# Laying q and k token by token on GpSimd before the DMA transposes of a fused attention and feed-forward kernel

## The chip, the cores and the metric

The kernel runs on one NeuronCore of a Trainium2 chip. The metric is the device time of one execution in microseconds (us), and of several executions the median counts. The engines are named as in the profile: PE is the tensor engine's matmuls and PEld its weight loads, DVE the vector engine, ACT the scalar engine, POOL is GpSimd, and SP is the engine that issues DMAs here, the transposing ones among them. An engine with a q behind its name (SPq) means its sequencer.

## The reference

For 8 batches, 12 heads, 448 tokens and a head width of 64, the kernel computes attention without a softmax, followed by a feed-forward block with a layer norm in front and a residual:

```python
scores = scale * np.matmul(q, k.transpose(0, 1, 3, 2))
attn = np.maximum(scores, 0.0) ** 2 / S
x = np.matmul(attn, v)                      # then heads side by side: (8, 448, 768)
xn = (x - mu) / np.sqrt(var + 1e-06) * g_ln
out = x + np.maximum(xn @ w_ch1, 0.0) @ w_ch2   # 768 -> 3072 -> 768
```

## The kernel before

**Groups.** A batch's twelve heads make six head pairs, and two head pairs (r = 0 and 1) make a group, so a batch has three groups (`G`) and the kernel 24. `load` brings q, k and v of a group in by a DMA issued on POOL, as tiles of 128 partitions (head of the pair, 64 token rows) by two times 448 elements. The 448 elements are seven tokens (`J`) of 64 elements, so a token and a head pair have a chunk of 64 columns each.

**Transposes.** The scores need q and k with the head width on the partitions. Batches 0 and 1 are transposed on PE (`transposes`). Batches 2 to 7 (groups 6 to 23, since `by_dma` is 2) are transposed by DMAs that SP issues, in blocks of 128 columns. A block of k holds two neighbouring chunks of one head pair (or, at the seam, the last of one pair and the first of the other), and they land on the partitions 0 to 63 and 64 to 127. The partner of a chunk of k is q's seven chunks of the same head pair on the same partitions, which is not where a plain transpose leaves all of them. So q is transposed twice, the second time shifted by 64 columns: `keys_dma` transposes 7 blocks of k (L227), `queries_dma` 8 blocks and 7 shifted blocks of q (L232 and L233), 22 blocks in three instructions a group. For the shift, q of batches 2 to 7 (and of batch 0) lies in `qbuf`, three fixed tiles with 64 columns of zeros on both sides (L101 to L104).

**Order.** The order of the instructions on each engine is the order in which the program writes them (a manual schedule): each engine takes its own in turn, and semaphores hold an instruction back until its inputs are there and its output buffer is free. After a start with batches 0 and 1 interleaved with their feed-forward part, the kernel goes through pairs of batches. `ffn1` (L479) of a pair runs alone; `ffn2` (L514) of that pair is interleaved with the attention of the next pair (`attention`, L408): between stretches of `ffn2` matmuls stands a bundle of three `item`s, each of which is the score matmuls (L270) of a group for one of its seven key blocks, and in some bundles also `product` of the group before (attention times v, L296). There are three such attention stages, 107 to 181, 236 to 312 and 367 to 441 us.

For each item ACT takes the ReLU out of the accumulator (L281) and DVE squares it (L282). After `product`, DVE scales the result (L303) and multiplies it by the gain (L309), and POOL adds up the chunks for the layer norm's mean (L324 and L327 in `chunks_summed`, and at a batch's end the conversion L330 and the subtraction L331). `centre` turns the sum into the mean on PE (L344), ACT copies it (L348) and DVE subtracts it (L350) in front of `ffn1`.

**In an attention stage, `transposed(n+1)` (L356) is called at the first item of group n.** It issues the loads of k for group n+4 and of q for group n+3, then the two transposes of q for group n+1 and the transpose of k for group n+2. The result of `queries_dma` has two buffers, that of `keys_dma` three. On SP these DMAs stand in one queue with the output DMAs (L529) and with `tokens` (L451), which transposes the attention's result of a pair, 42 blocks in one instruction.

Of the kernel before, what the change touches and what calls it, by code (L numbers as in the profile page):

```python
# [28 lines left out]
def kernel(  # L29
# [32 lines left out]
    J = S // HP  # L62
    NP = H // 2
    G = NP // 2
    NB = 2 * J + 1
    K1 = d_model // P
    K2 = d_ff // P
    S2 = 2 * S
# [7 lines left out]
    const = ctx.enter_context(tc.tile_pool(name="const", bufs=1))  # L76
# [21 lines left out]
        for n, t in (("q", q), ("k", k), ("v", v))  # L98
    }
    qkv = {}  # L100
    qbuf = [const.tile([P, 2 * S + 2 * D], bf16, name=f"q_sb{i}") for i in range(3)]  # L101
    for t in qbuf:
        nc.vector.memset(t[:, :D], 0.0)
        nc.vector.memset(t[:, D + 2 * S:], 0.0)  # L104

    groups = [(b, m) for b in range(B) for m in range(G)]

    def load(n, names):
        if n >= len(groups):
            return  # L110
        b, m = groups[n]
        for name in names:
            if b == 1 and name != "v":
                o = (2 * m + "qk".index(name)) * 2 * S
                t = hold[:, o:o + 2 * S].rearrange("p (r s) -> p r s", r=2)
            elif name == "q":
                t = qbuf[m][:, D:D + 2 * S].rearrange("p (r s) -> p r s", r=2)
            else:
                t = io.tile([P, 2, S], bf16, tag=name, name=name + "_sb", bufs=4 if name == "v" else 3)
            nc.gpsimd.dma_start(t, srcs[name][b][:, m:NP:G, :])  # L120
            qkv[name, b, m] = t
# [35 lines left out]
    ones = const.tile([P, P], bf16)  # L157
# [22 lines left out]
    def transposes(b, m):  # L180


        if b == 0:
            o = 12 * 1024 + m * 2 * J * P
            sb = early[:, o:o + 2 * J * P].rearrange("p (i c) -> p i c", c=P)
        elif m:
            o = (m - 1) * 2 * J * P
            sb = hold[:, o:o + 2 * J * P].rearrange("p (i c) -> p i c", c=P)
        else:
            sb = tpool.tile([P, NB, P], bf16, tag="qT", name="qT_sb")  # L190
        for i, n in enumerate(("q", "k")):
            src = qkv[n, b, m]
            if (b, m) == (0, 0):
                idle((36, 4)[i])
            if b == 0:
                ps = ps_mm.tile([P, 1024], bf16, tag="mm", name="tr_ps")
            else:
                ps = ps_sc.tile([P, 2, 1024], bf16, tag="sc", name="tr_ps")[:, 0]
            for j in range(J):
                for pr in range(2):  # L200
                    nc.tensor.transpose(  # L201
                        ps[pr * HP:(pr + 1) * HP, j * P:(j + 1) * P],
                        src[:, pr, j * D:(j + 1) * D], identity)
# [13 lines left out]

    kts = {}

    def keys_dma(n):
        if n >= len(groups):
            return
        kts[n] = tpool.tile([P, J, P], bf16, tag="kT", name="kT_sb", bufs=3)
        nc.sync.dma_start_transpose(kts[n], qkv[("k",) + groups[n]].rearrange("p r s -> p (r s)"))  # L227

    def queries_dma(n):
        m, kt = groups[n][1], kts[n]  # L230
        qt = tpool.tile([P, NB, P], bf16, tag="qT", name="qT_sb")
        nc.sync.dma_start_transpose(qt[:, 0:2 * J + 1:2, :], qbuf[m][:, :])  # L232
        nc.sync.dma_start_transpose(qt[:, 1:2 * J:2, :], qbuf[m][:, D:D + 2 * S])  # L233

        def queries(i, r):
            o = (2 * i + r) // J * J + 1 - r
            return qt[:, o:o + J]
        st[groups[n]] = {
            "q": queries,
            "k": lambda i: kt[:, i],  # L240
            "where": lambda pr, j: divmod(pr * J + j, 2),
            "attn": []}


# [6 lines left out]
    def busy(n):  # L251


        ps = ps_mm.tile([P, 512], fp32, tag="mm", name="busy_ps")
        for _ in range(n):
            nc.tensor.matmul(ps[:, :S], ones, qbuf[0][:, D:D + S], start=True, stop=True)

    def of(blk, b=0):
        o = b % 2 * S
# [2 lines left out]
    def scores(n, slots, blk):  # L262
        g, w = st[groups[n]], blk[1] * HP
        ps = ps_sc.tile([P, 2, 512], fp32, tag="sc", name="sc_ps")
        for o, i in enumerate(slots):
            for r in range(2):
                rows = slice(r * HP, (r + 1) * HP)
                for hh in range(2):
                    cols = slice(hh * HP, (hh + 1) * HP)
                    nc.tensor.matmul(  # L270
                        ps[cols, r, o * w:(o + 1) * w], g["k"](i)[rows, cols],
                        g["q"](i, r)[rows, blk[0]:sum(blk), cols], start=True, stop=True)
        if groups[n][0]:
            a = apool.tile([P, 2, 512], bf16, tag="attn", name="attn_sb")
        else:
            o = n_early[0] % 12 * 1024
            a = early[:, o:o + 1024].rearrange("p (r s) -> p r s", r=2)
            n_early[0] += 1
        since[0] = 0
        a = a[:, :, :len(slots) * w]  # L280
        nc.scalar.activation(a, ps[:, :, :len(slots) * w], ACTF.Relu)  # L281
        nc.vector.tensor_mul(a, a, a)  # L282
        for o, i in enumerate(slots):
            g["attn"].append(a[:, :, o * w:(o + 1) * w])
# [69 lines left out]
    by_dma = 2  # L354

    def transposed(n):  # L356

        if groups[n][0] < by_dma:
            transposes(*groups[n])
            return  # L360


        if n == by_dma * G:
            keys_dma(n)
        else:
            if n == by_dma * G + 1:
                load(n + 2, "k")
            load(n + 3, "k")
            load(n + 2, "q")
        queries_dma(n)  # L370
        keys_dma(n + 1)

    def attention_block(b, blk):

# [33 lines left out]
    def attention(bs):  # L408

        lo, hi = bs[0] * G, (bs[-1] + 1) * G
        seq = [(n, i) for n in range(lo, hi) for i in range(J)]

        def item(n, i):
            if i == 0 and n + 1 < len(groups) and groups[n + 1][0] >= by_dma:
                transposed(n + 1)  # L420
            scores(n, (i,), FULL)

        def product(n):
            values(n, FULL)
# [136 lines left out]
    interleave(ffn1_units(0, BLK[0][1]), attention_block(1, BLK[1][0]), 3, 1)  # L561
    interleave(ffn1_units(1, BLK[1][0]), attention_block(1, BLK[1][1]), 3, 1)
    tokens(0)
    for unit in ffn1_units(1, BLK[1][1]):
        unit()
    statistics(0, 0)
# [42 lines left out]
```

## Time and profile before

| | |
|---|---|
| median of the three runs | 557.33 us (556.60 to 557.53) |
| the profiled execution's own time | 557.41 us |
| its span, first to last instruction | 555.6 us |
| PE busy | 537.8 us, 97% of the span |
| DVE, ACT, POOL busy | 266.9, 257.8, 110.4 us |
| matmuls of `ffn2`, `ffn1`, scores of batches 2 to 7 | 227.4, 219.6, 34.8 us |
| granted tensor clock | 0.998 |

The busy times are the union of an engine's instructions. A group of instructions is told as line, engine, operation, output and inputs with their shapes, the count, then busy time and the mean duration of one, then the time that the engine sat idle just before them and what ended the idle time. The chain of work that ended last is followed back from the last instruction. The timeline gives start and duration of merged neighbours. A DMA has a second time, the one at which its data have landed.

### The profile page before, as it was taken

The numbers are of one execution on the slowest core, as the hardware profiler recorded it, in microseconds if no ns is written. First come the engines' busy times: TensorE is split into PE (matmuls) and PEld (weight loads), VectorE is DVE, ScalarE is ACT, GpSimd is POOL, SyncE is SP. The second block draws the span as 40 slices with busy tenths as digits, with TensorE's granted clock in tenths as the row PEclk, the third lists the DMA queues.
The fourth block names the chain that finished last, engine by engine and source line by source line (L and its number), as shares of the span: only waits on it lengthen the run. The fifth ranks groups of instructions, "written<-read, shape, count | busy, mean of one in ns | idle before, by whom it ended". The sixth has DMA issues, their size and how long they took to land.

```text
span 555.6 us, 10931 instructions
## 1 busy us (share of the span) xinstructions
PE 537.8 (97%) x4718; PEld 315.7 (57%) x4718; DVE 266.9 (48%) x510; ACT 257.8 (46%) x418; POOL 110.4 (20%) x136
## 2 busy tenths in 40 slices
PE   6879999999999999999999999999999999999996
PEld 5568778855555555555545555555555555556563
DVE  4856754178897350047777523016687670001111
ACT  4666766465643444455445344445555244430000
POOL 8334102014523310002524401001230400000000
PEclk9999999999999999999999999999999999999999
DMA  9999997969998990008998892005951240001122
GB/s 147 207 204 208 211 189 106 148 101 152 141 167 130 133 131 0 1 19 150 136 159 143 110 164 34 0 1 83 164 112 29 57 102 0 1 0 39 48 57 58
DMA packets 106896, 56.16 MB, mean 101 GB/s; under 512 B 77152, under 2 KB 103264, under 8 KB 106848
## 3 DMA queue, kind: packets, MB, share of 16 engines
q0 software_dynamic: 27520, 25.96, 32.7%
q1 hardware_dynamic: 79328, 29.51, 32.0%
q8 instruction: 37, 0.61, 0.4%
q14 instruction: 11, 0.09, 0.0%
HBM read 51.91 MB, written 11.01 MB: 113 GB/s over the span
## 4 chain that ended last, share of the span: by engine, by line
PE 91%; DMA 3%; ACT 2%; DVE 2%; SPq 0%; issue 0%; POOL 0%; POOLq 0%
PE o_ps L514 39%; PE h_ps L479 38%; PE sc_ps L270 6%; PE av_ps L296 5%; DMA qT_sb<-q_sb 2%; ACT early L281 2%; PE h_ps L498 1%; DMA k_sb<-in_k_dram 1%; PE sum_ps L344 1%; DVE early L282 1%; PE tr_ps L201 1%; DVE early L208 0%; SPq L232 0%; DVE o_sb L520 0%; DVE hT_sb L484 0%
## 5 line engine op out<-in xcount | busy, mean ns | idle before, releaser
L514 PE MATMUL o_ps<-w,hT_sb 128*128 128x384 bf16 x1344 | 227.4, 327 | 0.0
L479 PE MATMUL h_ps<-xc_sb,w 128*128 128x448 bf16 (+2 forms) x1368 | 219.6, 318 | 6.2 <-DVE hT_sb L484 5.3
L514 PEld LDWEIGHTS <-hT_sb 128*128 128x128 bf16 x1344 | 127.7, 98 | 97.5 <-issue 16.1
L479 PEld LDWEIGHTS <-w 128*128 128x128 bf16 x1368 | 128.5, 98 | 93.3 <-issue 10.0
L281 ACT ACTIVATE attn_sb<-sc_ps 128x896 bf16<-128x896 f32 (+4 forms) x150 | 126.5, 902 | 84.9 <-PE sc_ps L270 84.9
L486 ACT ACTIVATE hT_sb<-h_ps 128x448 bf16<-128x448 f32 (+2 forms) x212 | 102.5, 483 | 127.2 <-PE h_ps L479 126.7
L282 DVE TENSOR_TENSOR attn_sb<-attn_sb 128x896 bf16<-128x896 bf16 (+4 forms) x150 | 94.8, 640 | 54.2 <-ACT attn_sb L281 52.8
L520 DVE SCALAR_TENSOR_TENSOR o_sb<-o_ps,rstd_sb,xtok_sb 128x384 f32<-128x384 f32 x56 | 34.2, 611 | 55.6 <-PE o_ps L514 55.6
L464 DVE RECIPROCAL rstd_sb<-rstd_sb 128x1 f32<-128x1 f32 (+1 forms) x10 | 1.7, 169 | 96.6 <-ACT rstd_sb L463 96.6
L327 POOL TENSOR_TENSOR part_sb<-part_sb,xT_sb 128x448 f32<-128x448 f32 x24 | 29.5, 1229 | 71.1 <-DVE xT_sb L303 63.5
L458 DVE BATCH_NORM_STATS2 stats<-xtok_sb 128x6 f32<-128x384 bf16 x56 | 27.5, 533 | 33.4 <-DMA xtok_sb<-xT_sb 33.4
L350 DVE SCALAR_TENSOR_TENSOR xc_sb<-total_sb,g_mean,xc_sb 128x448 bf16<-128x448 f32 (+2 forms) x54 | 29.0, 606 | 21.1 <-ACT total_sb L348 21.1
L270 PE MATMUL sc_ps<-qT_sb,kT_sb 64*64 64x448 bf16 x504 | 34.8, 357 | 1.4 <-DMA qT_sb<-q_sb 1.4
L324 POOL TENSOR_TENSOR part_sb<-xT_sb 128x448 f32<-128x448 bf16 x6 | 6.6, 1105 | 140.3 <-DVE xT_sb L303 120.0
L296 PE MATMUL av_ps<-attn_sb,v_sb 64*64 64x448 bf16 (+2 forms) x672 | 32.1, 327 | 0.0
L309 DVE TENSOR_SCALAR xc_sb<-xT_sb,g_sb 128x448 bf16<-128x448 bf16 (+2 forms) x58 | 28.8, 544 | 1.0
L120 POOL DMA_DIRECT2D k_sb<-in_k_dram x21 | 15.1, 719 | 71.6 <-DMA kT_sb<-k_sb 40.3
L303 DVE TENSOR_SCALAR xT_sb<-av_ps 128x896 bf16<-128x896 f32 (+2 forms) x30 | 27.0, 899 | 4.5 <-PE av_ps L296 4.5
L296 PEld LDWEIGHTS <-v_sb 64*64 64x64 bf16 x840 | 22.8, 107 | 10.4 <-issue 2.0
L120 POOL DMA_DIRECT2D v_sb<-in_v_dram x24 | 17.5, 732 | 26.2 <-PE av_ps L296 23.9
L270 PEld LDWEIGHTS <-kT_sb 64*64 64x64 bf16 x504 | 11.5, 106 | 18.3 <-issue 14.9
L281 ACT ACTIVATE early<-sc_ps 128x768 bf16<-128x768 f32 (+3 forms) x24 | 18.3, 823 | 3.0 <-PE sc_ps L270 2.9
(56 smaller groups left out, 163.3 us busy)
## 6 DMA issues: line engine op xcount, KB each, us to landing
out_dram<-o_sb SPq DMA_DIRECT2D x56, 192.0 KB, 2.9
v_sb<-in_v_dram POOLq DMA_DIRECT2D x24, 224.0 KB, 4.6
q_sb<-in_q_dram POOLq DMA_DIRECT2D x21, 224.0 KB, 7.3
k_sb<-in_k_dram POOLq DMA_DIRECT2D x21, 224.0 KB, 6.3
w<-in_moe_w_ch_dram POOLq DMA_DIRECT2D x12, 384.0 KB, 14.5
w<-in_moe_w_ch_dram POOLq DMA_DIRECT2D x4, 1152.0 KB, 19.6
hold_sb<-in_q_dram POOLq DMA_DIRECT2D x3, 224.0 KB, 11.9
hold_sb<-in_k_dram POOLq DMA_DIRECT2D x3, 224.0 KB, 11.1
```

The source lines that it names most:

```text
L120: nc.gpsimd.dma_start(t, srcs[name][b][:, m:NP:G, :])
L270: nc.tensor.matmul(ps[cols, r, o * w:(o + 1) * w], g["k"](i)[rows, cols], g["q"](i, r)[rows, blk[0]:sum(blk), cols], start=True, stop=True)
L281: nc.scalar.activation(a, ps[:, :, :len(slots) * w], ACTF.Relu)
L282: nc.vector.tensor_mul(a, a, a)
L296: nc.tensor.matmul(ps[cols, hh, :w], v_sb[rows, pr, j * D:(j + 1) * D], g["attn"][i][rows, r, :], start=(j == 0), stop=(j == J - 1))
L309: nc.vector.tensor_scalar_mul(xc[b][:, c, of(blk)], xT[b // 2][:, c, of(blk, b)], g_sb[:, c:c + 1])
L327: nc.gpsimd.tensor_add(part[b], part[b], x[:, c])
L350: nc.vector.scalar_tensor_tensor(xc[b][:, c, of(blk)], total, g_mean[:, c:c + 1], xc[b][:, c, of(blk)], op0=ALU.mult, op1=ALU.add)
L479: nc.tensor.matmul(ps[:, :w], w1[:, c, ni * P:(ni + 1) * P], xc[b][:, c, of(blk)], start=(c == 0), stop=(c == K1 - 1))
L486: nc.scalar.activation(hT[pair][:, ni, o:o + w], ps[:, :w], ACTF.Relu)
L514: nc.tensor.matmul(ps[:, :DH], hT[pair][:, ki, t * P:(t + 1) * P], w2[:, ki, cols], start=(ki == 0), stop=(ki == K2 - 1))
L520: nc.vector.scalar_tensor_tensor(o_sb[t][:, cols].rearrange("p (c d) -> p c d", d=D), ps[:, :DH].rearrange("p (c d) -> p c d", d=D), rstd[ ...
```

## The change

For batches 2 to 7 POOL copies q and then k into one tile `both`, with the head pair inside the token (`p j r d` in place of `p r j d`). A block of 128 columns now holds the two chunks of one token, one for each head pair, and they fall on the same halves of the partitions for q and k alike. q is transposed once, and one DMA instruction transposes 14 blocks: 7 of q and 7 of k.

- `transposes_dma` takes the place of `keys_dma` and `queries_dma`. It makes two copies on POOL, issues the loads of q and k of the group three further on, and then one transpose on SP. `both` has one buffer, the transposed tile `qkT` three.
- In an attention stage it is called for group n+3 after the last item of group n, not for group n+1 at the first. The groups 6, 7 and 8 get theirs ahead of the first stage: group 6 at the place where its transposes stood before, 7 and 8 after `tokens(0)`.
- q of all batches but batch 1 lies in a pool of three buffers. `qbuf` and its six memsets are gone, and the filling matmuls `busy` read a tile of v instead.
- The order in which `values` takes the attention tiles becomes j = 0 to 6 for both head pairs (`where`).

```diff
-    NB = 2 * J + 1
+    NB = 2 * J
...
-    qbuf = [const.tile([P, 2 * S + 2 * D], bf16, name=f"q_sb{i}") for i in range(3)]
-    for t in qbuf:
-        nc.vector.memset(t[:, :D], 0.0)
-        nc.vector.memset(t[:, D + 2 * S:], 0.0)
...
-    kts = {}
-
-    def keys_dma(n):
+    def transposes_dma(n):
         if n >= len(groups):
             return
-        kts[n] = tpool.tile([P, J, P], bf16, tag="kT", name="kT_sb", bufs=3)
-        nc.sync.dma_start_transpose(kts[n], qkv[("k",) + groups[n]].rearrange("p r s -> p (r s)"))
-
-    def queries_dma(n):
-        m, kt = groups[n][1], kts[n]
-        qt = tpool.tile([P, NB, P], bf16, tag="qT", name="qT_sb")
-        nc.sync.dma_start_transpose(qt[:, 0:2 * J + 1:2, :], qbuf[m][:, :])
-        nc.sync.dma_start_transpose(qt[:, 1:2 * J:2, :], qbuf[m][:, D:D + 2 * S])
-
-        def queries(i, r):
-            o = (2 * i + r) // J * J + 1 - r
-            return qt[:, o:o + J]
+        both = tpool.tile([P, NB, 2, D], bf16, tag="both", name="both_sb", bufs=1)
+        for i, name in enumerate("qk"):
+            nc.gpsimd.tensor_copy(
+                both[:, i * J:(i + 1) * J],
+                qkv[(name,) + groups[n]].rearrange("p r (j d) -> p j r d", d=D))
+        load(n + 3, "qk")
+        sb = tpool.tile([P, NB, P], bf16, tag="qkT", name="qkT_sb", bufs=3)
+        nc.sync.dma_start_transpose(sb, both.rearrange("p b r d -> p (b r d)"))
         st[groups[n]] = {
-            "q": queries,
-            "k": lambda i: kt[:, i],
-            "where": lambda pr, j: divmod(pr * J + j, 2),
+            "q": lambda i, r: sb[:, 0:J],
+            "k": lambda i: sb[:, J + i],
+            "where": lambda pr, j: (j, pr),
             "attn": []}
...
-            nc.tensor.matmul(ps[:, :S], ones, qbuf[0][:, D:D + S], start=True, stop=True)
+            nc.tensor.matmul(ps[:, :S], ones, qkv["v", 0, 0][:, 0], start=True, stop=True)
...
-        if n == by_dma * G:
-            keys_dma(n)
-        else:
-            if n == by_dma * G + 1:
-                load(n + 2, "k")
-            load(n + 3, "k")
-            load(n + 2, "q")
-        queries_dma(n)
-        keys_dma(n + 1)
+        transposes_dma(n)
...
         def item(n, i):
-            if i == 0 and n + 1 < len(groups) and groups[n + 1][0] >= by_dma:
-                transposed(n + 1)
             scores(n, (i,), FULL)
+            if i == J - 1:
+                transposes_dma(n + G)
...
     tokens(0)
+    for n in range(1, G):
+        transposes_dma(by_dma * G + n)
```

More of the change, by code (lines that the diff above doesn't have):

```diff
@@ L115, in load @@
                 t = hold[:, o:o + 2 * S].rearrange("p (r s) -> p r s", r=2)
-            elif name == "q":
-                t = qbuf[m][:, D:D + 2 * S].rearrange("p (r s) -> p r s", r=2)
             else:
@@ L189, in transposes @@
         else:
-            sb = tpool.tile([P, NB, P], bf16, tag="qT", name="qT_sb")
+            sb = tpool.tile([P, NB, P], bf16, tag="qkT", name="qkT_sb", bufs=3)
         for i, n in enumerate(("q", "k")):
@@ L216, in transposes @@
             "attn": []}
-    kts = {}
-    def keys_dma(n):
+    def transposes_dma(n):
         if n >= len(groups):
             return
-        kts[n] = tpool.tile([P, J, P], bf16, tag="kT", name="kT_sb", bufs=3)
-        nc.sync.dma_start_transpose(kts[n], qkv[("k",) + groups[n]].rearrange("p r s -> p (r s)"))
-    def queries_dma(n):
-        m, kt = groups[n][1], kts[n]
-        qt = tpool.tile([P, NB, P], bf16, tag="qT", name="qT_sb")
-        nc.sync.dma_start_transpose(qt[:, 0:2 * J + 1:2, :], qbuf[m][:, :])
-        nc.sync.dma_start_transpose(qt[:, 1:2 * J:2, :], qbuf[m][:, D:D + 2 * S])
-        def queries(i, r):
-            o = (2 * i + r) // J * J + 1 - r
-            return qt[:, o:o + J]
+        both = tpool.tile([P, NB, 2, D], bf16, tag="both", name="both_sb", bufs=1)
[4 more added lines that the diff above has]
+        load(n + 3, "qk")
+        sb = tpool.tile([P, NB, P], bf16, tag="qkT", name="qkT_sb", bufs=3)
+        nc.sync.dma_start_transpose(sb, both.rearrange("p b r d -> p (b r d)"))
         st[groups[n]] = {
-            "q": queries,
-            "k": lambda i: kt[:, i],
-            "where": lambda pr, j: divmod(pr * J + j, 2),
+            "q": lambda i, r: sb[:, 0:J],
+            "k": lambda i: sb[:, J + i],
+            "where": lambda pr, j: (j, pr),
             "attn": []}
```

## The prediction, made before the changed kernel ran

> **What bounds the kernel now.** I read the busy times first, then the costliest groups, the three attention stages side by side, and last the waits and the chain where one stage differs. Busy times and groups:
>
> ```profile
> PE 537.8 (97%) x4718; PEld 315.7 (57%) x4718; DVE 266.9 (48%) x510; ACT 257.8 (46%) x418; POOL 110.4 (20%) x136
> ...
> L514 PE MATMUL o_ps<-w,hT_sb 128*128 128x384 bf16 x1344 | 227.4, 327 | 0.0
> L479 PE MATMUL h_ps<-xc_sb,w 128*128 128x448 bf16 (+2 forms) x1368 | 219.6, 318 | 6.2 <-DVE hT_sb L484 5.3
> ...
> L270 PE MATMUL sc_ps<-qT_sb,kT_sb 64*64 64x448 bf16 x504 | 34.8, 357 | 1.4 <-DMA qT_sb<-q_sb 1.4
> ```
>
> PE is the bound. The change leaves every matmul as it is, so it can win only PE's idle time, and of that only the 1.4 us before the score matmuls hang on a transpose. The busy times by stage (PE, PEld, DVE, ACT, POOL, then clock, DMA share and GB/s):
>
> ```profile
> 106.89:181.22 74.33, 74.33 (x675) 40.32 (x674) 59.24 (x107) 38.20 (x51) 24.36 (x27) 1.00 0.90 140
> 236.07:311.97 75.90, 74.53 (x676) 40.33 (x674) 51.90 (x80) 37.33 (x45) 22.95 (x25) 1.00 0.85 119
> 366.83:441.15 74.32, 74.32 (x675) 40.32 (x674) 52.12 (x80) 37.22 (x45) 15.64 (x15) 1.00 0.44 78
> ```
>
> The three stages hold the same PE work, and the second is 1.57 us longer. The chain goes through this place (start, duration, work):
>
> ```profile
> 268.82 1.50 SPq L232
> 270.37 10.63 DMA qT_sb<-q_sb
> 281.09 0.57 PE sc_ps L270 x8
> ```
>
> The shifted q of group 16, issued at 270.37, landed 10.63 us later, and PE stood until then.
>
> **What the change removes.** The stall: 75.90 - 74.33 = 1.57 us. It goes because the transpose is now issued when the group three earlier has its scores: a group takes 74.33 / 6 = 12.4 us, so about 25 us before use, less POOL's copies and the landing. The row nearest to one transpose of 14 blocks is `tokens` (42 blocks, 7.8 to 18.2 us, median 16.6): a third is 2.6 to 6.1 us. Even the 10.63 us above would fit twice. The six memsets (85 ns each) run before 1.2 us, while PE waits for the first q: nothing. Three SP instructions a group become one; SP is on the chain only here: nothing more. What is late next: no other group waited.
>
> **What it adds.** 18 times two copies on POOL of 128x896 bf16. No such row exists. The nearest are POOL's conversion and the vector engine's instructions beside it (first fence POOL, second DVE):
>
> ```profile
> 148.09 0.83 POOL L330 CAST two_sb<-part_sb 128x448 bf16<-128x448 f32 x1
> 149.00 1.29 POOL L331 TENSOR_TENSOR two_sb<-part_sb,two_sb 128x448 bf16<-128x448 f32 x1
> ```
>
> ```profile
> 147.81 2.96 DVE L282 TENSOR_TENSOR attn_sb<-attn_sb 128x896 bf16<-128x896 bf16 x3 [0.16 <-ACT attn_sb L281]
> ```
>
> The conversion takes 0.56 us beside an idle DVE and 0.83 here. A one-element POOL memset takes 0.10, so twice the elements make 0.10 + 2 x 0.46 = 1.0 us; without a fixed part 1.1; from the contended 0.83, 1.7. I take 1.0 to 1.1, since the 0.83 holds waiting. And there is contention: three squarings take 2.96 us here, where they are 0.63 each elsewhere, while POOL's two instructions were stretched by 0.28 and 0.26 us. The two engines keep each other out. The Trainium skill (page "SBUF — State Buffer", section "Who interferes with whom") calls this an exclusive lock that the later one waits for in full; the trace agrees, with a squaring that ended 0.48 us after L331 did.
>
> POOL's load, per group: 2.1 us of copies on top of 2.1 of DMA issues and 1.1 to 4.8 of sums, of 12.4. It fits, and `both` with its one buffer only makes a copy wait for the transpose before it, issued a group earlier. Behind the copies in POOL's queue stand the loads of q and k (needed three groups later), the sums for `centre` (in the second batch of a pair 2.3 us early at 185.8) and the loads of v. All keep their cover.
>
> So what counts is where a copy meets a DVE instruction that PE needs soon. I find three places.
>
> *Near 94 us.* The copies of group 7 follow in POOL's queue the load of v that ends at 91.33 (before, loads of k stood there), if group 6's transpose has landed. That one follows the v load of 82.32: copies to 85.2, landing 2.6 to 6.1 us later, 87.8 to 91.3.
>
> ```profile
> 91.33 1.43 POOL L120 DMA_DIRECT2D k_sb<-in_k_dram  x2
> ```
>
> ```profile
> 92.65 2.06 DVE L350 SCALAR_TENSOR_TENSOR xc_sb<-total_sb,g_mean,xc_sb 128x192 bf16<-128x192 f32 x6 [1.26 <-ACT total_sb L348]
> ```
>
> ```profile
> 94.01 1.65 PE L498 MATMUL h_ps<-xc_sb,w 128*128 128x192 bf16 x18
> ```
>
> The six L350 start 0.33 us apart; PE wants the sixth at 94.01 + 5 x 0.25 = 95.25 and has it at 94.71. With copies of 1.05 us they run 91.4 to 93.5, the first L350 ends at 93.8 instead of 93.07 (about 0.27 after the copy), the sixth at 95.4: PE stalls 0.1 to 0.3. If the transpose lands later, the second copy comes in between the L350, and 1.1 us is the worst. I take 0.3. Its lower bound is 0.
>
> *Third product of each stage.* The copies follow the v load that ends at 138.96, and meet these:
>
> ```profile
> 139.04 0.63 DVE L282 TENSOR_TENSOR attn_sb<-attn_sb 128x896 bf16<-128x896 bf16 x1 [0.66 <-ACT attn_sb L281]
> 139.85 0.63 DVE L282 TENSOR_TENSOR attn_sb<-attn_sb 128x896 bf16<-128x896 bf16 x1 [0.18 <-ACT attn_sb L281]
> 140.66 0.63 DVE L282 TENSOR_TENSOR attn_sb<-attn_sb 128x896 bf16<-128x896 bf16 x1 [0.18 <-ACT attn_sb L281]
> ```
>
> ```profile
> 141.78 1.50 PE L296 MATMUL av_ps<-attn_sb,v_sb 64*64 64x448 bf16 x28
> ```
>
> Taking turns with copies of 1.05, the last squaring ends at about 142.5 instead of 141.29. The product reads that tile from its 25th matmul of 28 on, at 141.78 + 24/28 x 1.32 = 142.9 (before, from the 21st: that is what the new `where` gives). Cover 0.4 us: cost 0, with 0.75 a stage at copies of 1.7.
>
> *Near 87 us.* Group 6's copies delay an L484 from 86.20 to about 86.8; PE wants its accumulator at 87.46: cost 0, with 0.6 at copies of 1.7.
>
> **Sum.** 557.41 (the profiled execution, 555.6 of span and 1.8 around it) - 1.57 + 0.3 = 556.14. The median of the runs is 0.08 lower, so 556.1.
>
> **The rivals.**
>
> *A, most is given back.* Group 6's transpose lands after 91.3, or the copies take about 1.35 us. For it: the loads of group 9 now go out beside that transpose, and DMAs were busy there. Against: `tokens` in quiet took 7.8 us for three times the blocks. Late landing costs 1.1: 556.9. Copies of 1.35 cost 0.52 near 94 and 0.11 in each third product, 0.85: 556.7. The Trainium skill's "GPSIMD Engine Reference" (section "Performance versus the Vector engine") gives 1.8 cycles an element at 1.2 GHz as its best case, which by my estimate is 1.34 us for a copy and would make this rival the rule; the conversion's clean 0.56 us for 448 elements stands against it (0.67 by that figure).
>
> *B, slower: GpSimd's copies hold the port that the squarings need.* At 1.7 us a copy the stalls are 1.16 near 94, 0.75 in each of three third products, and 0.6 near 87: 4.0 us, against 1.57 won: 557.33 + 2.4 = 559.8. Near 1.45 us a copy the sum turns from gain to loss. For it: the copies read bf16 in an order of 64-element pieces that no row shows, and DVE is busy 59.24 of 74.33 us in the first stage. Against: the clean conversion.
>
> *C, the transposes do not come earlier*, since one `both` buffer, POOL's order and SP's queue chain them: PE would wait as before, 557.3. Against: 25 us of lead against some 10 for the whole chain.
>
> **How the numbers follow.** Forecast 0.50 (555.5 to 556.6), A 0.28, B 0.17, C 0.05. A difference of about 0.2%, 1.1 us, is what a measurement of this kernel can tell from none, and the forecast stands just beyond it: faster needs 556.2 or less. I give that 0.42 (most of the forecast), same 0.38 (its rest, A, C), slower 0.20 (B and tails). The range starts at 555.4 (stall gone, nothing added, and the scatter of the runs) and reaches past A to 558.8, which leaves most of B out.
>
> **What would show it.** The wait of the score matmuls on a DMA is gone, and the second stage is as long as the third. POOL's copies show about 1.0 us beside an idle DVE, up to 1.9 with waiting. The transpose lands within 6 us or so. Squarings and L350 next to copies are stretched. PE has a new idle time in front of the L498 near 94 us, below 0.5. I am wrong if copies take 1.45 us or more clean, if products wait for squarings, or if the sums in front of `centre` come late.

## The result and the profile after

The changed kernel takes 561.03 us (median, 558.87 to 565.09) beside 557.48 us (556.06 to 560.19) of the kernel before, a ratio of 1.0065 with a 95% interval of 1.0039 to 1.0090: slower by 3.5 us. Measured once more beside other kernels it was 1.0063 (1.0035 to 1.0091). The forecast of 556.1 us and its range up to 558.8 us both missed.

The profiled execution took 560.70 us, its span is 558.9 us, 3.3 us longer than before. Three parts of its page, busy times, chain and costliest groups:

```profile
PE 540.2 (97%) x4718; PEld 317.6 (57%) x4718; DVE 292.0 (52%) x504; ACT 257.6 (46%) x418; POOL 142.6 (26%) x172
...
PE 82%; DVE 13%; ACT 2%; issue 1%; DMA 1%; POOL 0%; ACTq 0%; POOLq 0%
...
L491 PE MATMUL o_ps<-w,hT_sb 128*128 128x384 bf16 x1344 | 227.7, 326 | 2.7 <-DVE o_sb L497 2.6
...
L269 DVE TENSOR_TENSOR attn_sb<-attn_sb 128x896 bf16<-128x896 bf16 (+4 forms) x150 | 113.4, 778 | 39.4 <-ACT attn_sb L268 38.7
```

POOL is busy 32 us longer (its 36 copies take 36.6), and DVE 25 us longer, though it got no work. The squarings (L269, before L282) went from 640 to 778 ns each, 18.6 us in sum, and the multiplications by the gain (L296, before L309) take 7.0 us more. The chain, which ran through PE for 91% of the span, now runs through DVE for 13%. And PE waits 2.6 us for an accumulator (`o_ps`, L491, before L514), which DVE frees with L497 (before L520); before there was no such wait.

The three attention stages of the changed kernel (PE, PEld, DVE, ACT, POOL, then clock, DMA share and GB/s):

```profile
108.09:185.80 77.71, 74.86 (x676) 40.41 (x674) 68.72 (x104) 38.10 (x51) 37.06 (x43) 1.00 0.79 125
240.66:315.44 74.78, 74.51 (x675) 40.41 (x674) 60.00 (x80) 37.22 (x45) 33.92 (x37) 1.00 0.75 107
370.38:444.70 74.32, 74.32 (x675) 40.31 (x674) 54.97 (x80) 37.22 (x45) 18.73 (x18) 1.00 0.32 58
```

The second stage has lost its stall, as forecast (75.90 to 74.78). The first went from 74.33 to 77.71 with DVE busy 68.72 us of it. Where the 2.6 us arise stands in the timeline of the changed kernel (start, duration, work):

```profile
176.57 0.74 POOL L114 DMA_DIRECT2D v_sb<-in_v_dram  x1
176.68 2.92 DVE L269 TENSOR_TENSOR attn_sb<-attn_sb 128x896 bf16<-128x896 bf16 x1
...
177.31 0.94 POOL L219 COPY both_sb<-q_sb 128x896 bf16<-128x896 bf16 x1
178.18 0.94 POOL L219 COPY both_sb<-k_sb 128x896 bf16<-128x896 bf16 x1
...
179.52 0.60 DVE L497 SCALAR_TENSOR_TENSOR o_sb<-o_ps,rstd_sb,xtok_sb 128x384 f32<-128x384 f32 x1
...
180.18 1.14 PE L491 MATMUL o_ps<-w,hT_sb 128*128 128x384 bf16 x6 [2.57 <-DVE o_sb L497]
```

One squaring takes 2.92 us instead of 0.63. It starts beside the DMA issue for v, it does not get in between the two copies, and it ends 0.48 us after the second. Neither copy is stretched. Behind the squaring in DVE's queue stands L497, and behind that PE. It is the second such squaring in a row: one at 165.54 took 2.93 us, and DVE had not one idle moment between the two.

The starts of the same matmul in the two traces, laid side by side, give the whole difference: 0.4 us at the start, 0.7 near 95 us, 0.4 and 0.3 near 155 and 170, 2.8 at 180, 1.55 won at the old stall (281 us), 0.4 near 310, and 0.15 less over the rest, in sum 3.3.

### The profile page after: what moved, and what is told of

The parts are those of the page before. It is cut to its first block, busy times and chain, and to the rows that moved or that the text cites. A ratio compares the mean times of both kernels' runs of the same rounds, so it can differ in the third digit from the quotient of the medians.

```text
span 558.9 us, 10894 instructions
## 1 busy us (share of the span) xinstructions
PE 540.2 (97%) x4718; PEld 317.6 (57%) x4718; DVE 292.0 (52%) x504; ACT 257.6 (46%) x418; POOL 142.6 (26%) x172
## 4 chain that ended last, share of the span: by engine, by line
PE 82%; DVE 13%; ACT 2%; issue 1%; DMA 1%; POOL 0%; ACTq 0%; POOLq 0%
PE h_ps L456 37%; PE o_ps L491 32%; PE sc_ps L257 5%; DVE attn_sb L269 5%; PE av_ps L283 4%; DVE xc_sb L296 2%; ACT early L268 2%; DVE xT_sb L290 1%; PE h_ps L475 1%; DVE xc_sb L337 1%; DVE o_sb L497 1%; PE tr_ps L195 1%; DMA k_sb<-in_k_dram 1%; PE sum_ps L331 1%; DVE early L269 1%
## 5 line engine op out<-in xcount | busy, mean ns | idle before, releaser
L491 PE MATMUL o_ps<-w,hT_sb 128*128 128x384 bf16 x1344 | 227.7, 326 | 2.7 <-DVE o_sb L497 2.6
L456 PE MATMUL h_ps<-xc_sb,w 128*128 128x448 bf16 (+2 forms) x1368 | 219.6, 318 | 6.2 <-DVE hT_sb L461 5.3
L491 PEld LDWEIGHTS <-hT_sb 128*128 128x128 bf16 x1344 | 127.8, 98 | 100.2 <-issue 19.0
L456 PEld LDWEIGHTS <-w 128*128 128x128 bf16 x1368 | 128.7, 98 | 93.0 <-issue 10.0
L269 DVE TENSOR_TENSOR attn_sb<-attn_sb 128x896 bf16<-128x896 bf16 (+4 forms) x150 | 113.4, 778 | 39.4 <-ACT attn_sb L268 38.7
L497 DVE SCALAR_TENSOR_TENSOR o_sb<-o_ps,rstd_sb,xtok_sb 128x384 f32<-128x384 f32 x56 | 34.2, 610 | 55.2 <-PE o_ps L491 55.2
L337 DVE SCALAR_TENSOR_TENSOR xc_sb<-total_sb,g_mean,xc_sb 128x448 bf16<-128x448 f32 (+2 forms) x54 | 30.4, 631 | 19.8 <-ACT total_sb L335 19.8
L314 POOL TENSOR_TENSOR part_sb<-part_sb,xT_sb 128x448 f32<-128x448 f32 x24 | 26.5, 1105 | 51.1 <-DVE xT_sb L290 50.2
L257 PE MATMUL sc_ps<-qkT_sb 64*64 64x448 bf16 (+2 forms) x560 | 36.7, 348 | 0.0
L296 DVE TENSOR_SCALAR xc_sb<-xT_sb,g_sb 128x448 bf16<-128x448 bf16 (+2 forms) x58 | 35.8, 664 | 1.0
L283 PE MATMUL av_ps<-attn_sb,v_sb 64*64 64x448 bf16 (+2 forms) x672 | 32.5, 327 | 0.4 <-DVE attn_sb L269 0.3
L283 PEld LDWEIGHTS <-v_sb 64*64 64x64 bf16 x840 | 23.2, 108 | 11.1 <-issue 2.6
L219 POOL COPY both_sb<-q_sb 128x896 bf16<-128x896 bf16 x18 | 17.7, 981 | 21.9 <-DMA qkT_sb<-both_sb 21.9
L257 PEld LDWEIGHTS <-qkT_sb 64*64 64x64 bf16 x560 | 12.7, 105 | 17.6 <-issue 14.2
```

The lines of the kernel that those rows point to most:

```text
L257: nc.tensor.matmul(ps[cols, r, o * w:(o + 1) * w], g["k"](i)[rows, cols], g["q"](i, r)[rows, blk[0]:sum(blk), cols], start=True, stop=True)
L283: nc.tensor.matmul(ps[cols, hh, :w], v_sb[rows, pr, j * D:(j + 1) * D], g["attn"][i][rows, r, :], start=(j == 0), stop=(j == J - 1))
L296: nc.vector.tensor_scalar_mul(xc[b][:, c, of(blk)], xT[b // 2][:, c, of(blk, b)], g_sb[:, c:c + 1])
L337: nc.vector.scalar_tensor_tensor(xc[b][:, c, of(blk)], total, g_mean[:, c:c + 1], xc[b][:, c, of(blk)], op0=ALU.mult, op1=ALU.add)
L456: nc.tensor.matmul(ps[:, :w], w1[:, c, ni * P:(ni + 1) * P], xc[b][:, c, of(blk)], start=(c == 0), stop=(c == K1 - 1))
L491: nc.tensor.matmul(ps[:, :DH], hT[pair][:, ki, t * P:(t + 1) * P], w2[:, ki, cols], start=(ki == 0), stop=(ki == K2 - 1))
```

## The experiments

Three theories stood. **P**: POOL's copies keep DVE out, DVE falls behind and PE waits. **S**: the new order and time of loads and transposes on POOL's and SP's queues costs it. **C**: the changed start costs tensor clock, since the trace shows the clock at half for 3.41 us from 11.49 us on. Executions of one kernel scatter by several us here, the kernel before from 556 to 564 us, so ratios are given with their intervals, and the reason for each is read from the trace.

### Without the copies

Each loaded tile is transposed directly.

```diff
-        for i, name in enumerate("qk"):
-            nc.gpsimd.tensor_copy(both[:, i * J:(i + 1) * J], ...)
-        load(n + 3, "qk")
...
-        nc.sync.dma_start_transpose(sb, both...)
+        for i, name in enumerate("qk"):
+            nc.sync.dma_start_transpose(sb[:, i * J:(i + 1) * J], qkv[(name,) + groups[n]]...)
+        load(n + 3, "qk")
```

> The changed kernel without POOL's copies: two transposes a group take q and k as they were loaded, 7 blocks each, at the same places three groups ahead (the layout stays head pair by head pair, so the scores pair other rows; the work on every engine is the same but for the copies). Theory P (POOL's copies keep DVE from the SBUF port, DVE falls behind and PE waits): squarings at 0.63 us, no wait of PE on DVE near 94, 171, 180 and 312 us, and the transposes still early, so 557.5 - 1.57 = 555.9 (555.2 to 556.6). Rival S (the loss comes from the new order and time of loads and transposes on POOL's and SP's queues): 560 to 561, as the changed kernel. Rival C (the loss is a lower tensor clock after the changed start): 560 to 561 too, with stretches of half clock.

Measured: 560.61 us, 1.0041 (1.0012 to 1.0071). By the time alone that is S or C. The trace says otherwise: squarings take 679 ns in the mean (640 before, 778 with the copies), the first stage is 74.61 us, and what costs is a wait that the edit itself put in. POOL in that kernel's timeline:

```profile
186.83 0.71 POOL L114 DMA_DIRECT2D q_sb<-in_q_dram  x1 [6.83 <-DMA qkT_sb<-q_sb]
...
188.36 2.15 POOL L312 TENSOR_TENSOR part_sb<-part_sb,xT_sb 128x448 f32<-128x448 f32 x2
...
192.30 0.35 PE L329 MATMUL sum_ps<-two_sb,ones 128*128 128x448 bf16 x1 [0.76 <-POOL two_sb L316]
```

Without the copies the loads of q and k must wait until the transpose has read their tile, and POOL's sums stand behind them, so that PE's sums wait for POOL at the ends of three batches, 3.5 us in all. This profiled execution also had a half clock of 10.24 us from 14.13 us on, and was 4.5 us behind the kernel before by 25 us. The run settles nothing about P; that takes a kernel with every instruction and wait in place (below, the short copies).

### The kernel before, with copies that nobody reads

```diff
             load(n + 4, "v")
+            for g in (n + 2, n + 3):
+                if g < len(groups):
+                    t = qkv[("v",) + groups[g]]
+                    nc.gpsimd.tensor_copy(t, t)
```

> The kernel before, with two copies of 128x896 bf16 on POOL after each load of v in the attention stages, of v tiles onto themselves: the port is used as in the changed kernel, and nothing else moves. Theory P: a squaring next to them takes up to 2.9 us, DVE is full in the first stage, PE waits some 2.6 + 0.3 + 0.3 + 0.4 us for it on top of the old stall, 560 to 562. Rival S: copies alone do nothing, 557.0 to 558.0. Rival C: the same, 557.0 to 558.0.

Measured: 560.47 us, 1.0028 (0.9999 to 1.0057). That is in P's range, but the interval just reaches no difference, so here the trace has to tell. Squarings of 2.93 us appear five times, and the first two stages grow from 74.33 and 75.90 us to 76.71 and 76.23:

```profile
108.22:184.93 76.71, 75.35 (x676) 40.47 (x674) 68.17 (x107) 38.34 (x51) 33.16 (x37) 1.00 0.95 137
```

Copies alone bring the held squarings and longer stages into a kernel whose transposes and loads are untouched. Its start is untouched as well, and the trace still has a half clock of 3.41 us at 12.27 us: C's stretch does not come from the changed start.

### A load between the two copies

```diff
-        load(n + 3, "qk")
+            load(n + 3, name)
```

> The changed kernel with the load of q for the group three ahead between the two copies instead of behind both. Theory P in the form that DVE and POOL take turns at every POOL instruction: a squaring is held for one copy at most (up to about 1.6 us in place of 2.9), the loss shrinks to 557 to 559.5. Theory P in the form that a copy waiting behind a DMA issue in POOL's queue already holds the port: the hold lasts from the issue before the first copy to the end of the second, a squaring takes up to 3.6 us, 561 to 564. Rivals S and C: 561, unchanged.

Measured: 558.09 us, 1.0005 (0.9976 to 1.0033). Timeline of that kernel:

```profile
256.99 0.74 POOL L114 DMA_DIRECT2D v_sb<-in_v_dram  x1
257.10 4.01 DVE L269 TENSOR_TENSOR attn_sb<-attn_sb 128x896 bf16<-128x896 bf16 x2
257.73 0.94 POOL L219 COPY both_sb<-q_sb 128x896 bf16<-128x896 bf16 x1
258.96 0.71 POOL L114 DMA_DIRECT2D q_sb<-in_q_dram  x1 [0.30 <-POOL both_sb L219]
```

Where a load stands between the copies (the last two groups have none left to issue), a held squaring takes 2.04 us: one DMA issue, one copy and its own rest. DVE gets in after the first copy. The first stage is 74.95 us. The time is in the range of the first form of P, but the squarings are longer than that form's 1.6 us and shorter than the 3.6 us of the second: neither has the length right.

### Less of DVE's other work

The row statistics leave the first stage, and one tile's are used for all.

```diff
...
-            if pair == 0 and h == 0 and p == 1 and t + 1 < NT:
-                statistics(pair, t + 1)
-            if pair == 0 and h == 1 and p == 2 and t + 1 < NT:
-                roots(pair, t + 1, t + 2)
```

> The changed kernel without the layer norm's statistics of the first pair's tiles 1 to 6 (one tile's reciprocal deviation stands for all seven), which takes some 8.6 us of DVE work out of the first attention stage and nothing else. Theory P: the first stage becomes like the second, its waits of 2.6 + 0.3 + 0.3 us vanish while the copies stay: 557.5 to 558.8. Rival S: 560 to 561, since no queue is touched. Rival C: 560 to 561.

Measured: 559.17 us, 1.0015 (0.9988 to 1.0043), 0.4 us outside what P allowed. Most of the loss went with DVE's work, by the middle of the intervals; but there is still a wait for an accumulator:

```profile
PE o_ps L491 <- DVE o_sb L497: 1.9, 2, 1.7
```

So both count. Before the wait at 179 us in this trace DVE was idle for 0.69 us at 170.21 and then one hold of 2.91 us was enough to cost PE 1.74 us. In the changed kernel's first trace DVE had not caught up from the hold before, and PE waited 2.57 us.

### Short copies

Same instructions, order, waits, loads and transposes; each copy writes one block of the seven, into a tile that is zeroed once at the start.

```diff
...
-                both[:, i * J:(i + 1) * J], qkv[(name,) + groups[n]]...
+                both[:, i * J:i * J + 1], qkv[(name,) + groups[n]][:, :, 0:D]...
```

> Left out: each copy writes one block of 128 columns instead of seven; the tile that is transposed is zeroed once at the start and otherwise zero, so the scores are of zeros. The instructions, their order, the waits, the loads and the one transpose of 14 blocks a group are those of the changed kernel. P (the length of GpSimd's copies is the cost): a copy takes 0.2 us instead of 0.94, no squaring is held beyond 1.7 us, the accumulator wait of 2.6 us at 180 us is gone, and the time is 555.8 to 557.2 us (the changed kernel less its stalls, with the 1.57 us of the old stall won). S (order and time of loads and transposes): as the changed kernel, 560 to 561. C (the start and its half clock): 560 to 561, with the half-clock stretch near 11 us in the trace.

Measured: 556.11 us, 0.9961 (0.9942 to 0.9981). P's number, and S and C are out as the cause: the order of loads and transposes and the changed start, which they name, are still in this kernel. One doubt was left, since TensorE multiplied zeros. So the copies of group 6 were made in full and the tile kept:

> Left out: after the copies of group 6, each copy writes only its first block of 128 columns, so that the other blocks stay those of group 6; scores are of real numbers, and not of zeros as with the short copies before. It tells the length of the copies from the numbers that TensorE multiplies. P: the copies of group 6 cost what they cost in the changed kernel, the rest nothing: 556 to 557.2 us. If the gain of the short copies came from the zeros (a clock that is disturbed less): 559 to 561.

Measured: 556.34 us, 0.9960 (0.9934 to 0.9985). It is the length of the copies, and not the zeros. Its first two stages:

```profile
106.82:181.16 74.34, 74.34 (x676) 40.33 (x674) 61.73 (x106) 38.18 (x51) 30.70 (x45) 1.00 0.84 127
236.09:310.41 74.32, 74.32 (x675) 40.31 (x674) 54.50 (x80) 37.22 (x45) 28.16 (x37) 1.00 0.77 107
```

### The copies on another engine

DVE copies, or in a second kernel ACT with `nc.scalar.copy`, and the copies of groups 7 and 8 are moved to where no transpose should be waited for.

```diff
-            nc.gpsimd.tensor_copy(
+            nc.vector.tensor_copy(
...
-    for n in range(1, G):
-        transposes_dma(by_dma * G + n)
-    for unit in ffn1_units(1, BLK[1][1]):
+    for i, unit in enumerate(ffn1_units(1, BLK[1][1])):
+        if i == 6:
+            transposes_dma(by_dma * G + 1)
         unit()
+    transposes_dma(by_dma * G + 2)
```

> The copies on the vector engine, and those of groups 7 and 8 issued six units into the feed-forward block that follows and behind it, so that they wait for no transpose. P: the vector engine does a copy in 0.63 us or less (a squaring of that size with two operands takes 0.63), 1.3 us a group, and nothing is held by GpSimd but what it was before: 555.8 to 557.5 us. If instead it is the vector engine's load in the first stage that decides (59.24 of 74.33 us busy before, 1.3 us a group more), waits for o_sb and av remain there: 557.5 to 559. S, C: 560 to 561.

Measured: 562.07 us, 1.0058 (1.0035 to 1.0081): a miss of all three theories. DVE's timeline in that kernel:

```profile
114.77 0.62 DVE L219 COPY both_sb<-q_sb 128x896 bf16<-128x896 bf16 x1 [14.51 <-DMA qkT_sb<-both_sb]
...
119.17 1.15 DVE L269 TENSOR_TENSOR attn_sb<-attn_sb 128x896 bf16<-128x896 bf16 x2
```

The copy of group 8 waited 14.5 us until the transpose of group 7 had read `both`; that transpose stood behind the 42 blocks of `tokens` in SP's queue. The squarings stood behind the copy in DVE's queue, and PE lost 4.6 us near 118 us, part of it to a half clock that came 1.4 us after the wait. Everywhere else the trace agrees with P: copies of 0.61 us, no held squaring. My move was not late enough.

> As the one on the vector engine, with the copies on ScalarE. P: 0.9 us a copy by the rows of its activations (917 ns for 128x896), 1.9 us a group behind which the next activation of the scores stands; it is busy 38 of 74 us in a stage, so 556 to 558 us. S, C: 560 to 561.

Measured: 562.61 us, 1.0082 (1.0050 to 1.0113), again outside every range. ACT's 0.94 us a copy was as expected, but two in a row delay what stands behind them: PE waits 3.4 us for ACT in `ffn1` (L456) and 1.2 us in the products (L283).

> Copies on GpSimd with a load between them, and groups 7 and 8 moved as in the other two. P: the stall near 96 us (0.4 to 0.8 in the kernel with a load between) is gone, and 557.0 to 558.0 us remain, as the vector engine is still kept out for one copy and one DMA issue at a time (2.04 us squarings). S, C: 560 to 561.

Measured: 559.06 us, 1.0012 (0.9991 to 1.0033), 1 us above what was expected. There was no stall near 95 us left to win once a load stood between the copies, and this execution's first stage was 75.98 us.

Then the mend: groups 6 to 8 stay on POOL (with the load between), the copies issued inside the stages go to DVE.

```diff
+    def transposes_dma(n, by=None):
-            nc.gpsimd.tensor_copy(
+            (by or nc.gpsimd).tensor_copy(
-        load(n + 3, "qk")
+            load(n + 3, name)
...
-                transposes_dma(n + G)
+                transposes_dma(n + G, nc.vector)
```

> The copies of groups 6 to 8 on GpSimd with a load between them; those of the groups from 9 on, which are issued inside the attention stages, on the vector engine, where by then no transpose is waited for. P: 0.61 us a copy on the vector engine, no squaring held beyond 1.5 us after 130 us, no wait for an accumulator or product in the stages, the 1.57 us of the old stall won: 555.7 to 557.3 us, below both kernels. If the vector engine's load in the first stage decides: waits for o_sb stay, 558 to 560. S, C: 560 to 561.

Measured: 556.20 us, 0.9962 (0.9937 to 0.9987), faster than both kernels, and the three stages are equal (the first two shown):

```profile
107.66:181.99 74.33, 74.33 (x676) 40.31 (x674) 63.86 (x116) 38.09 (x51) 28.72 (x33) 1.00 0.85 125
236.85:311.18 74.33, 74.33 (x675) 40.31 (x674) 57.48 (x92) 37.22 (x45) 25.78 (x29) 1.00 0.72 112
```

The third takes 74.32 us. DVE does 1.2 us of copies a group and PE does not notice. The change as such, earlier transposes and fewer blocks, was worth what the prediction said; the copies on POOL in their place behind a DMA issue took it away.

### No DMA issue ahead of the copies

In the changed kernel POOL's queue after a product is: sums, load of v, copy, copy. Here the load goes ahead of the sums.

```diff
         if blk == FULL:
+            load(n + 4, "v")
             chunks_summed(b, m)
...
             values(n, FULL)
-            load(n + 4, "v")
```

> The load of v goes out ahead of GpSimd's sums of the product instead of behind them, so that no DMA issue stands directly ahead of the first copy. If a queued copy keeps the vector engine out from the DMA issue ahead of it on: squarings beside the copies end after at most 2.3 us (two copies, 1.87, and its own 0.43) instead of 2.9, and the time is 558.5 to 560.5 us. If GpSimd's instructions that follow each other without a gap are one hold: sums and copies together make squarings of 3 to 4.5 us, and 561 to 564. If neither, as the changed kernel: 2.9 and 560 to 561.5.

Measured: 557.49 us, 0.9975 (0.9951 to 0.9999), below its forecast. The copies are the same, on the same engine, and most of the loss is gone: by the edge of its interval it is faster than the kernel before. What is left in its trace is the 0.8 us near 95 us, and first two stages of 74.66 and 74.82 us. Its timeline:

```profile
128.94 1.88 DVE L269 TENSOR_TENSOR attn_sb<-attn_sb 128x896 bf16<-128x896 bf16 x2
129.35 0.99 POOL L219 COPY both_sb<-q_sb 128x896 bf16<-128x896 bf16 x1 [0.47 <-DMA qkT_sb<-both_sb]
130.28 1.33 POOL L219 COPY both_sb<-k_sb 128x896 bf16<-128x896 bf16 x1
...
130.81 0.59 DVE L497 SCALAR_TENSOR_TENSOR o_sb<-o_ps,rstd_sb,xtok_sb 128x384 f32<-128x384 f32 x1
```

Here the engines do take turns: both squarings, a reciprocal and L497 are done while the copies run, and the copies stretch instead (k's 1.23 us in the mean of 18, against 1.05). No DVE instruction beside a copy exceeds 1.45 us in the stages, less than the 2.3 I had expected; the only hold left, 2.33 us at 83.6, is that of group 6, whose copies still follow a DMA issue. Five of the pairs start right behind a sum, without waiting for a transpose, and they take turns too: it is not the wait that lets DVE in.

### The changed kernel again

> The changed kernel once more, beside the other three on the same chip and on its own traces: 560 to 561.5 us by every theory. P, in the trace: squarings of up to 2.9 us beside the copies and PE waits of 1 to 4 us in sum in the first attention stage. C: a half-clock stretch near 11 us in it.

Measured: 561.92 us, 1.0063 (1.0035 to 1.0091); but its profiled execution, at 558.15 us, lost only 0.2 us in the first two stages. Three further executions, and one of the kernel before, tell what decides:

> One more execution of the changed kernel. The first traced one had a first stage of 77.7 us, the second of 74.6. If it is decided by whether a pair of copies stands directly behind the DMA issue of v (the transpose before it has landed by then) or starts by itself when the transpose lands: pairs directly behind a DMA issue take 1.81 us and hold one squaring for 2 us or more, the others are stretched to 2 us or more with squarings of at most 1.35; the excess of the stages over 74.3 us grows with the number of the first kind. If it is the clock: the excess goes with half-clock stretches in the stages.

> A further execution of the changed kernel, with the two expectations of the look before it: pairs of copies directly behind a DMA issue with a squaring held 2 us or more and a longer stage for each, or half-clock stretches inside the stages.

> A further execution of the changed kernel, with the same two expectations: the stages' excess over 74.3 us goes with the number of pairs of copies directly behind a DMA issue, or with half-clock stretches inside the stages.

The first two stages of the execution at 558.15 us:

```profile
108.79:183.36 74.57, 74.53 (x675) 40.48 (x674) 65.47 (x104) 38.09 (x51) 37.01 (x42) 1.00 0.90 125
238.28:312.61 74.33, 74.33 (x676) 40.34 (x674) 58.73 (x80) 37.22 (x45) 33.26 (x37) 1.00 0.75 105
```

Of the three further ones, at 562.62, 560.71 and 563.31 us, the stages that lost most are the first of 79.31 us, the second of 76.22 us and the first of 80.06 us. Two of these rows:

```profile
108.55:187.86 79.31, 76.47 (x675) 40.89 (x674) 68.94 (x104) 38.10 (x51) 37.05 (x43) 0.98 0.81 125
```

```profile
239.20:315.42 76.22, 74.48 (x676) 40.32 (x674) 60.55 (x80) 37.22 (x45) 33.71 (x37) 1.00 0.70 110
```

The five traces of the changed kernel hold 90 pairs of copies. In 41 the first copy starts when the transpose ahead of it lands: no DVE instruction beside these takes more than 1.45 us, and most pairs are stretched from 1.81 to 1.9 to 2.6 us. In 49 the pair follows a DMA issue directly: 44 run at 1.81 us, and 40 of these hold a DVE instruction for 1.86 to 2.93 us (beside the other four DVE has nothing to do); the remaining five are stretched and take turns. Squarings held for more than 2 us in the first two stages, and those stages' excess over twice 74.33 us:

| execution | held over 2 us | excess, us |
|---|---|---|
| 558.15 us | 2 | 0.24 |
| 560.71 us | 3 | 2.21 |
| 560.70 us (the first one) | 5 | 3.83 |
| 563.31 us | 6 | 5.73 |
| 562.62 us | 7 | 5.28 |

The last two hold a half clock of 3.41 us inside the first stage (0.98 in the clock column), 1.5 and 0.4 us after the wait for the accumulator ended: a cost that comes on top of the wait. Which pair is held matters too. The one ahead of the first stage's last product, with the accumulator behind it, cost 2.8 us in the three executions in which DVE was already behind (560.70, 562.62 and 563.31 us); where DVE had been idle before, the like place of the second stage cost 1.9 us (560.71 us). So both expectations hold, and in these two the half clock follows the held squarings.

Of the 24 executions of the changed kernel, the eight with a granted clock of 0.998 or more took 558.87 to 561.90 us, median 559.5; the 18 such of the kernel before that were measured beside the second half have a median of 557.9. So some 1.7 us of the loss are there at full clock, and the rest goes with a lower one. The traces show half clocks after the new waits and at the start; how much of the latter the change brings is open. By 25 us the five traces of the changed kernel are 0.3 to 1.4 us behind the first one of the kernel before, its second trace is 0.1 behind, but its variant with copies, which has the same start, 1.3.

> One more execution of the kernel before: the wait of the second stage on the shifted q's transpose between 0 and 3 us, as the transposes land sooner or later; first and third stage 74.3 us. A half-clock stretch at the start adds about 1 to 1.7 us where it is.

Measured: 557.41 us, with stages of 74.33 and 75.79 us and no half clock at the start: the old stall is the same in both traces.

## Why the prediction was wrong

**The stall.** Right: 1.55 us won at 281 us in the side by side, 1.57 forecast, and nothing was late next. The kernel that keeps this part and little else (short copies) measures 556.11 us. That it meets the forecast's 556.1 to the digit is luck, since the forecast held 0.3 us of contention and the executions scatter by more.

**The size of the copies.** Right: 1.0 to 1.1 us forecast, means of 0.98 and 1.05 us, 0.93 to 0.94 where nothing stretches them. The prediction's estimate by the figure of the Trainium skill's "GPSIMD Engine Reference", section "Performance versus the Vector engine", 1.34 us, was too long for this copy.

**The step that failed: "Taking turns with copies of 1.05".** The prediction took from one place of the trace (three squarings beside POOL's conversion and subtraction) that an instruction of DVE gets in after each one of POOL. It does so where POOL's pair starts from an idle queue or behind a sum. Directly behind a DMA issue it does not: the squaring that starts beside the issue waits for the rest of it and for both copies, 0.63 + 1.81 + its own 0.48 = 2.92 us. In the trace of before POOL has no compute instruction directly behind a DMA issue at all, but for a memset at 2.8 us, so no row could show it; the order in the code did show that the change would make such pairs (load of v, then copies). With the load of v moved, the same copies behind a sum held nothing beyond 1.45 us: it is the place in the queue. In the kernel without copies, where sums came to stand behind a DMA issue, one sum held a squaring in the same way, for 2.17 us (0.63 of the issue, 1.04 of the sum, its own 0.49), but between that sum and the next DVE got in. Why two copies in a row do not let it in there stays open. The prediction even named the DMA issue that the copies follow and did not ask whether that changes anything. The Trainium skill's "SBUF — State Buffer", section "Who interferes with whom", speaks of a lock for one whole instruction; what was measured here reaches over a DMA issue and two instructions.

**Third product of each stage, cost 0.** At that place it was nearly right: no loss near 143 us in the first trace, 0.4 us in two of the four others. What failed is that only three places were counted. The prediction looked at what waits for a squaring: the product. What cost 2.8 us was the instruction behind it in DVE's queue, L497, and the accumulator that it frees, ahead of the sixth product, and the prediction put nothing there. It said what is queued behind POOL's copies, and not what is queued behind DVE's held squaring.

**Near 94 us, 0.3, worst 1.1.** The place was right, the size 0.7. The late case came, which is the condition of rival A, though at 0.7 and not 1.1 us: group 6's transpose landed at 93.9 us, the copies ran from 93.93 to 95.86, in the middle of the six L337 (before L350). Timeline of the changed kernel:

```profile
93.61 2.79 DVE L337 SCALAR_TENSOR_TENSOR xc_sb<-total_sb,g_mean,xc_sb 128x192 bf16<-128x192 f32 x4
93.93 0.93 POOL L219 COPY both_sb<-q_sb 128x896 bf16<-128x896 bf16 x1 [2.31 <-DMA qkT_sb<-both_sb]
...
96.12 0.74 PE L475 MATMUL h_ps<-xc_sb,w 128*128 128x192 bf16 x6 [0.59 <-DVE xc_sb L337]
```

**Near 87 us, 0.** Right: no loss there, though the squaring beside group 6's copies was held to 2.36 us.

**The rivals.** The outcome was rival B's, whose name fits, "GpSimd's copies hold the port that the squarings need", but its condition was wrong: it made the copy's length decide, with 1.45 us as the break-even, and by that condition the measured 0.94 would have spoken against it. C, late transposes, did not come: the wait of the score matmuls on a DMA is gone. The signs named in the prediction as fatal included "if products wait for squarings"; two did in the first trace, for 0.3 and 0.4 us (at 171 and 312 us), but the long wait was that for an accumulator.

**Not in the prediction: the clock.** At 281 us, PE's old wait of 1.4 us was followed by no half clock in either trace of the kernel before. Near 180 us two of three waits of 2.57 us were. By these traces a new wait's price in this kernel is its length, or that plus an estimated 1.7 us (half of 3.41).

Which of the two it is, the traces nearly tell. In all 18 of them every stretch at one clock, the first and the last of an execution apart, lasts a whole number of times 3.41 us. Of the intervals of 3.41 us counted this way, the one ahead of the half clock held 2.57 us of idle PE in the execution at 562.62 us and 1.97 us in that at 563.31 us; in the first execution the wait fell across two, with 1.13 and 1.44 us, and the clock stayed. Over all traces no interval at full clock with less than 1.46 us of idle PE was followed by a half clock, and every one with 2.03 us or more was; in between both happened. The idle times are estimates, since the ends of matmuls are modelled, and no run tested this.

## What to carry to other kernels

Between two engines that keep each other out, count holds and not busy time: ask for each instruction of the one what stands directly ahead of it in its queue, and for each instruction of the other what stands behind it. Long instructions on POOL right behind a DMA issue were the bad place here; behind a compute instruction, or inside the stages on DVE, the same work cost little. And an edit meant to remove a cost can put a wait in its place (both the kernel without copies and the first one with copies on DVE did): to test for such a cost, keep the instructions and shorten them.

## What the runs showed of the hardware that was not expected

- POOL's copies directly behind a DMA issue on POOL (not all, 40 of 49 pairs) held one DVE instruction until both had ended, up to 2.93 us; with a load between the copies 2.04; behind a sum or an idle queue at most 1.45. In the first trace the held squaring ended 0.48 to 0.49 us after the second copy, whether it started 0.63 or 0.29 us before the first (2.92 and 2.58 us) or 0.08 us after its start (2.21 us): what it did ahead of the copies gained it nothing. That a copy counts from the time it stands behind the DMA issue would explain it; the traces show when, not how.
- A POOL copy of 128x896 bf16 in pieces of 64 elements takes 0.94 us, on ACT 0.94 to 0.95, on DVE 0.61.
- The tensor clock fell to half for 3.41 us after waits of PE of 2.57 us (0.4 and 1.5 us after their end) in two executions, and did not in a third. The Trainium skill's "TensorE: Matmul & The Clock Gate", section "Part 1: The HAM clock gate", puts the fall after an idle window of about 3.4 us; here the intervals of 3.41 us ahead of these falls were idle for 2.57 and 1.97 us only.
- One transpose of 14 blocks lands 3.8 to 12.4 us after its issue (median 7.0, first trace). A pair starts directly behind a DMA issue if the transpose ahead of it has landed by then, so which pairs are held changes from one execution to the next, and with it much of the difference between 558 and 563 us.
